# 64x64 output blocks, halved score masks and a scaling on GpSimd in a planned attention and MoE kernel

## Chip, cores, metric

One core of a Trainium2 chip runs the whole kernel. The metric is the device time of one execution in microseconds (us). The kernel before took 293.16 us, the median of three runs (292.2 to 295.71).

## What is computed

The reference chains three layers. First comes linear attention with decay, in blocks of 64 positions, for 2 batches, 8 heads, 768 positions and head size 64:

```python
for b in range(nb):                       # 12 blocks of 64
    intra = (qb @ kb.T * Dmask) @ vb      # Dmask: lam^(i-j) where i >= j, else 0
    inter = (qb * lam_pow) @ kv_state     # what earlier blocks left
    out[block] = intra + inter
    kv_state = lam**64 * kv_state + (kb * rev_pow).T @ vb
```

The scores of a block are masked only against keys of the same block; everything earlier comes through the 64x64 state of each head. Then follow `x = hardswish(x @ w_in) @ w_out` (512 to 2048 to 512, 1536 rows, the hidden rows are called g) and a soft mixture of 8 experts (`phi`, `w1`, `w2`) with two softmaxes over the logits `x @ phi`.

## The kernel before

**Attention tiles.** Twelve tiles t, six per batch, of 128 positions, that is, two chunks of 64. For each tile TensorE transposes q and k (`f_tr`, line 807, into PSUM `pt`), ScalarE copies both to SBUF `tr` (`f_ev`, line 824), and VectorE multiplies the transposed q, read from PSUM, by the powers of lambda `lamq` into `trd` (`f_trd`, line 830). The scores `ps` are 32 matmul records of 64x64 (`f_sc`, line 877). VectorE masks them in two instructions (`f_pm`, line 889): each score chunk is broadcast into both chunk columns and multiplied by `dec`, whose off-diagonal chunk is zero, so that `pm` holds 128 query columns per head and takes a whole buffer. GpSimd scales k (`f_kd`, line 863), TensorE forms the new states' products (`f_pv`, line 902), GpSimd decays the states (`f_sm`, line 947) and VectorE adds (`f_st`, line 960). The tile's output `px` (`f_px`) is 8 products of 128 keys by 64 by 128 queries (line 913; two records each) and then 16 small products with the states, 64x64 (line 921). ScalarE and VectorE split `px` into a high and a low part `x` (lines 938, 942).

**Matmul units.** 48 units (tile, quarter of `w_in`), 12 matmuls each of 128x512 (`h_unit`, line 1038), then ScalarE (line 1052) and VectorE (line 1058) make g. `w_in` and `w_out` arrive as 64-bit numbers and are converted by ScalarE and VectorE (lines 599 to 649; the low parts of two quarters by GpSimd, line 649). g reaches its transposed form through a VectorE transpose (line 1121) and four transfers from SBUF to SBUF (`f_move`, line 1131, tiles gq) for 5 of the 6 tile pairs.

**The end.** 64 transfers of 512 KB bring the experts' weights e (lines 1341, 1351, 1365); TensorE multiplies them as they land (lines 1559, 1593), and the rows of the output are formed (line 1662), copied and stored.

**Order.** Nothing is scheduled at run time. Every piece of work is an `op` with a number; `ORDER` lists all 974 numbers, and each engine runs its own in that order (`Plan.run`). The DMA transfers are issued in that order too, nearly all by SyncE (SP); those in `BY_ACT` by ScalarE. SBUF consists of 50 buffers of 4 KB per partition; each is handed from op to op by the plan, so a transfer of e waits at the head of SP's queue until the work that still reads its buffer is done. The sums in the plan (`cost`, `SWITCH`) choose which freed buffer an op gets.

Of the kernel before, what the change touches and what calls it, by code (L numbers as in the profile page):

```python
# [258 lines left out]
def attn_moe_softmoe_kernel(  # L259
# [237 lines left out]
    for item in CFG["loads"].split():
        i = int(item[1:])
        if item[0] in "qkv":
            load_qkv(item[0], i)  # L500
        elif item[0] == "t":
            for x in "qkv":
                load_qkv(x, i)
        elif item[0] == "w":
            load_w_in(i // 4, i % 4)
        elif item[0] == "W":
            for kt in range(KT):
                load_w_in(i, kt)
        elif item[0] == "p":
            ops["phi"] = load(load_phi, 65536, eff=0.4)  # L510
        elif item[0] == "D":
            each = {"SP": 600, "ACT": 700, "POOL": 1300}[CFG["decq"]]
            ops["pw_d"] = load(
                store_pw, 8192, deps=[pw_done], rel=[rp_buf], eng=CFG["decq"],
                each=440 if CFG["decq"] == "SP" else 800, free=CFG["decq"] == "SP",
            )
            ops["dec"] = [
                load(
                    load_dec(g), KB512 / 4, deps=[ops["pw_d"], zero],
                    eff=0.5, rows=32, eng=CFG["decq"], each=each, free=CFG["decq"] == "SP",  # L520
                )
                for g in range(2)
            ]
        elif item[0] == "o":
            load_wo_raw(i)
        else:
            for kk in range(4 * i, 4 * i + 4):
                load_wo_raw(kk)
# [1208 lines left out]
```

## Time and profile before

| | |
|---|---|
| median of three runs | 293.16 us |
| profiled execution, device time | 292.0 us |
| its span in the trace | 290.2 us |
| granted TensorE clock, mean | 0.993 |
| TensorE busy | 271.1 us, 93% |
| VectorE busy | 200.4 us, 69% |
| ScalarE busy | 122.9 us, 42% |
| GpSimd busy | 43.0 us, 15% |
| moved by DMA | 78.49 MB, 270 GB/s over the span |

The span is what the trace covers; the device time holds 1.8 us more. The ends of matmuls are modelled and overlap their successors, so a TensorE that is shown busy throughout may still have short gaps; what a block of matmuls costs is read from start to start. DMA shares are means over 16 engines.

### The profile page before, as it was taken

To read this page: it belongs to the slowest core of one execution; us is meant where nothing else is said; L and a number is where in the kernel's file an instruction comes from. 1 tells how busy PE (TensorE), PEld (TensorE's weight loads), DVE (VectorE), ACT (ScalarE), POOL (GpSimd) and SP (SyncE) were. 2 spreads that over 40 slices of the span, in tenths; PEclk is the share of its full clock that TensorE was granted. 3 is DMA by queue.
4 is the path that set the end of the run, shared out by engine and by line. 5 is a ranking of instruction groups with operands and counts; after the bars stand their busy time and mean duration, and the time that the engine had idled before them with its cause. 6 is when DMAs were issued, how large, how long until landed. Compare 5 with 4: busy or idle time off the path is not lost.

```text
span 290.2 us, 8501 instructions
## 1 busy us (share of the span) xinstructions
PE 271.1 (93%) x3532; PEld 205.4 (71%) x3532; DVE 200.4 (69%) x336; ACT 122.9 (42%) x237; POOL 43.0 (15%) x58
## 2 busy tenths in 40 slices
PE   7897999999999999999999999989999987999880
PEld 7786788778777888876677566768776665577570
DVE  5688899999999999977995976886124232160152
ACT  3475789988676562021332041403213511111250
POOL 6145323803062100000100202000000000000000
PEclk9999999999999999999999999999999999999997
DMA  8999889998688775686857899999999999999987
GB/s 183 266 249 287 225 242 311 350 354 241 185 248 244 201 199 118 149 210 167 208 134 173 186 265 269 309 330 306 338 403 390 357 368 382 412 405 377 288 274 217
DMA packets 79350, 78.49 MB, mean 270 GB/s; under 512 B 42952, under 2 KB 68048, under 8 KB 79312
## 3 DMA queue, kind: packets, MB, share of 16 engines
q1 hardware_dynamic: 77088, 76.50, 86.9%
q10 hardware_dynamic: 2224, 1.45, 1.9%
q8 instruction: 28, 0.46, 0.7%
q14 instruction: 10, 0.08, 0.1%
HBM read 60.10 MB, written 3.15 MB: 218 GB/s over the span
## 4 chain that ended last, share of the span: by engine, by line
PE 57%; DVE 10%; DMA 9%; issue 3%; ACT 2%; SPq 1%; DVEq 0%; ACTq 0%
PE h L1038 31%; DMA e<-in_moe_w_dram 6%; PE lg L1144 4%; PE po L1593 4%; PE pd L1259 4%; PE p L1559 3%; DVE tmp_o L613 2%; DMA wraw<-in_moe_w_in_dram 2%; DVE wo_f L620 2%; PE px L913 1%; PE pg L1103 1%; DVE g L1058 1%; PE pt L807 1%; PE w2p L751 1%; PE pt L1662 1%
## 5 line engine op out<-in xcount | busy, mean ns | idle before, releaser
L1038 PE MATMUL h<-whi,x 128*128 128x512 f32 x384 | 122.5, 400 | 2.1 <-DVE g L1058 1.9
L1038 PEld LDWEIGHTS h<-whi,x 128*128 128x128 f32 x384 | 69.6, 188 | 19.5 <-DVE g L1058 4.0
L1038 PE MATMUL h<-wlo,x 128*128 128x512 f32 x192 | 75.0, 391 | 0.0
L1052 ACT ACTIVATE g<-h,half_b 128x512 f32<-128x512 f32 x48 | 33.0, 692 | 58.2 <-PE h L1038 44.5
L1058 DVE SCALAR_TENSOR_TENSOR g<-g,h 128x512 f32<-128x512 f32 x48 | 32.3, 679 | 20.1 <-ACT g L1052 20.0
L1038 PEld LDWEIGHTS h<-wlo,x 128*128 128x128 f32 x192 | 36.0, 188 | 8.0
L1121 DVE STREAM_TRANSPOSE gb<-g 128x1024 f32<-128x1024 f32 x20 | 40.5, 2038 | 1.5 <-PE pd L1259 0.8
L947 POOL TENSOR_TENSOR states<-states,lamq 128x256 f32<-128x256 f32 x20 | 14.0, 702 | 89.9 <-DVE states L960 44.0
L863 POOL TENSOR_TENSOR vd<-qk,rev 128x512 f32<-128x512 f32 x12 | 13.5, 1128 | 40.4 <-DMA qk<-in_k_dram 16.0
L1593 PE MATMUL po<-e,ht 128*32 128x128 f32 (+1 forms) x384 | 16.6, 310 | 2.2 <-DMA e<-in_moe_w_dram 1.1
L1578 DVE STREAM_TRANSPOSE ht<-hsi 128x256 f32<-128x256 f32 x8 | 5.1, 646 | 19.5 <-ACT hsi L1570 19.5
L889 DVE TENSOR_TENSOR pm<-ps,dec 128x512 f32<-128x512 f32 x24 | 16.3, 680 | 1.7 <-DMA gq<-gb 1.4
L1559 PE MATMUL p<-e,hsi 128*32 128x256 f32 x256 | 15.9, 380 | 1.6 <-PE psi L1431 1.0
L824 ACT COPY tr<-pt 128x512 f32<-128x512 f32 x24 | 13.5, 586 | 7.4 <-DVE trd L830 3.9
L726 DVE STREAM_TRANSPOSE wb<-wo_f 128x1024 f32<-128x1024 f32 x8 | 16.4, 2049 | 0.1
L807 PE MATMUL pt<-ident,qk 128*128 128x128 f32 x96 | 15.6, 302 | 0.7 <-DMA qk<-in_q_dram 0.4
L1593 PEld LDWEIGHTS po<-e,ht 128*32 128x32 f32 x384 | 11.7, 110 | 6.0 <-DMA e<-in_moe_w_dram 1.6
L807 PEld LDWEIGHTS pt<-ident,qk 128*128 128x128 f32 x96 | 12.0, 153 | 4.3 <-issue 2.2
L1559 PEld LDWEIGHTS p<-e,hsi 128*32 128x32 f32 x256 | 9.1, 110 | 6.8 <-PE psi L1431 1.2
L620 DVE SCALAR_TENSOR_TENSOR tmp_i<-tmp_i 128x512 int32<-128x512 int32 x16 | 11.2, 708 | 3.2 <-ACT tmp_i L606 3.2
L620 DVE SCALAR_TENSOR_TENSOR wo_f<-tmp_o 128x512 int32<-128x512 int32 x16 | 13.3, 851 | 0.0
L913 PE MATMUL px<-pm,vd 128*64 128x128 f32 x192 | 13.1, 279 | 0.0
(116 smaller groups left out, 348.4 us busy)
## 6 DMA issues: line engine op xcount, KB each, us to landing
e<-in_moe_w_dram SPq DMA_DIRECT2D x64, 512.0 KB, 8.4
gq<-gb SPq DMA_DIRECT2D x72, 128.0 KB, 3.1
wraw<-in_moe_w_in_dram SPq DMA_DIRECT2D x16, 512.0 KB, 6.3
wo_raw<-in_moe_w_out_dram SPq DMA_DIRECT2D x16, 512.0 KB, 5.9
wq<-wb SPq DMA_DIRECT2D x32, 128.0 KB, 3.0
qk<-in_k_dram SPq DMA_DIRECT2D x24, 128.0 KB, 4.5
qk<-in_q_dram SPq DMA_DIRECT2D x24, 128.0 KB, 4.7
vd<-in_v_dram SPq DMA_DIRECT2D x12, 256.0 KB, 6.0
```

Of the source, the lines that this page charges most:

```text
L620: DVE.scalar_tensor_tensor(out=lw if dst is None else dst(), in0=hp, scalar=3, in1=lw, op0=ALU.logical_shift_left, op1=ALU.bitwise_or,)
L726: DVE.transpose(out=x.rearrange("p q d c f -> p c d q f"), in_=y.rearrange("p c (d t q) -> p c d q t", d=KT, q=4),)
L807: PE.transpose(p[:, a], x[:, i, 2 * a : 2 * a + 2].rearrange("p a d -> p (a d)"), ident,)
L889: DVE.tensor_tensor(out=T["pm", t][:, h], in0=T["ps", t][g][:, 0][:, :, None, :].broadcast_to((128, NPAIR, 2, Q)), in1=T["dec"][:, h], op= ...
L913: PE.matmul(px[kt // 2][rows(h2), kt % 2], lhsT=vd[:, 0, h], rhs=P[:, h], start=kt % 2 == 0, stop=False,)
L947: POOL.tensor_tensor(out=states[:, (n + 1) % 4], in0=states[:, n % 4], in1=T["lamq"][:, :, C - 1 : C].broadcast_to((128, NPAIR, Q)), op=AL ...
L1038: PE.matmul(ph, lhsT=xt[:, a, kt], rhs=T[w, n, part][:, kt % 2], start=i == 0, stop=i == 3 * KT - 1,)
L1052: ACT.activation(T["g", tp, n][:, i], T["h", t, n], AF.Relu, bias=half_b, scale=1.0 / 6.0)
L1058: DVE.scalar_tensor_tensor(out=to, in0=to, scalar=1.0, in1=T.pop(("h", t, n)), op0=ALU.min, op1=ALU.mult,)
L1121: DVE.transpose(out=x.rearrange("p q c i t -> p i c q t"), in_=T["g", tp, n].rearrange("p i (c t q) -> p i c q t", c=4, q=4),)
L1559: PE.matmul(p1[32 * j : 32 * j + 32], lhsT=T["sit"][:, b4], rhs=T["e1", e, b4][:, 256 * j : 256 * j + 256], start=b4 == 0, stop=b4 == 3,)
L1593: PE.matmul(T["po", hf][32 * qd : 32 * qd + 32], lhsT=T["ht", e // 4][:, e % 4, b8], rhs=T["e2", e, b8 // 2][:, b8 % 2, lo:hi] if e < WHOL ...
```

## The change

Five edits in the attention part, and a new order:

- `pm` holds only the equal chunks: 64 query columns per head instead of 128, one VectorE instruction of 128x256 per half instead of 128x512. It shares a buffer `tp` with `trd`; `dec` shares one with `lamq`. The zeroing of `dec` by GpSimd goes.
- `trd` is made by GpSimd from the SBUF copy `tr` instead of by VectorE from PSUM.
- In `f_px` the state products come first and open the accumulation; the 8 products of 128x64x128 become 16 of 64x64x64, in two halves of 8 with a drain of TensorE between them. In the first half the rows of the array match the rows used by the state products of the same PSUM tile; in the second they are the other ones.
- The two `dec` transfers wait for `lamq` (whose buffer they share) instead of for the zeroing. The ops `first`, `rev`, `lamq` are numbered ahead of the loads.
- `ORDER` is replaced (973 entries). With the shift in numbers undone (from 78 on, a number is one lower than before): SP starts with three of the four parts (512 KB each) of the first quarter of `w_in` and then k and q of tile 0, where it started with one part; two loads of e stand ahead of v and of k of tiles 9 and 10, and 16 loads of e instead of 14 stand ahead of the last transfers of gq; the products of tile 11's `px` and the first logits of pair 4 stand ahead of the units of tiles 8 and 9 in quarter 3; the logits of pair 3 stand behind seven units instead of behind the softmax sums of pair 2.

```diff
-            T["dec"] = bass.AP(
-                r.tensor, r.offset + Q - 1, [list(r.ap[0]), [2 * Q, H], [Q, 2], [-1, Q]]
-            )
+            T["dec"] = bass.AP(r.tensor, r.offset + Q - 1, [list(r.ap[0]), [Q, H], [-1, Q]])
...
-    zero = op("POOL", 1000, zero_dec, [pw_done], take=[ring_buf("dec")])
...
         def f_trd():
-            T["trd", t] = rtile([128, NPAIR, C], f"trd{t}")
-            DVE.tensor_tensor(out=T["trd", t], in0=T["pt", t, 0], in1=T["lamq"], op=ALU.mult)
+            T["tp", t] = rtile([128, 2, 512], f"tp{t}")
+            T["trd", t] = T["tp", t][:, 0].rearrange("p (a c) -> p a c", a=NPAIR)
+            POOL.tensor_tensor(
+                out=T["trd", t], in0=T["tr", t][:, 0], in1=T["lamq"], op=ALU.mult
+            )
...
-                if ("pm", t) not in T:
-                    T["pm", t] = rtile([128, H, 2, Q], f"pm{t}")
+                T["pm", t] = T["tp", t][:, 1].rearrange("p (h c) -> p h c", h=H)
                 h = slice(NPAIR * g, NPAIR * g + NPAIR)
                 DVE.tensor_tensor(
-                    out=T["pm", t][:, h],
-                    in0=T["ps", t][g][:, 0][:, :, None, :].broadcast_to((128, NPAIR, 2, Q)),
-                    in1=T["dec"][:, h], op=ALU.mult,
+                    out=T["pm", t][:, h], in0=T["ps", t][g][:, 0], in1=T["dec"][:, h],
+                    op=ALU.mult,
                 )
...
-            for kt in range(KT):
-                for h2 in range(2):
-                    h = 2 * kt + h2
-                    PE.matmul(
-                        px[kt // 2][rows(h2), kt % 2], lhsT=vd[:, 0, h], rhs=P[:, h],
-                        start=kt % 2 == 0, stop=False,
-                    )
+            first = 0 if c > 0 else 1
             for a in range(2):
-                for i in range(0 if c > 0 else 1, 2):
+                for i in range(first, 2):
                     for b in range(2):
                         for h2 in range(2):
                             PE.matmul(
                                 px[b][rows(h2), a, rows(i)],
                                 lhsT=states[rows(b), (2 * c + i) % 4, 2 * a + h2],
                                 rhs=T["trd", t][rows(b), 2 * a + h2, rows(i)],
-                                start=False, stop=a == i == 1,
+                                start=a == 0 and i == first, stop=False,
+                            )
+            for k in range(2):
+                if k:
+                    PE.drain()
+                for a in range(2):
+                    for b in range(2):
+                        for h2 in range(2):
+                            i, h = b ^ k, NPAIR * b + 2 * a + h2
+                            PE.matmul(
+                                px[b][rows(h2), a, rows(i)], lhsT=vd[rows(i), 0, h],
+                                rhs=P[rows(i), h], start=False, stop=k == a == 1,
                             )
...
-                "DVE", 610, f_trd, [tq, ops["lamq"]], prio, take=[b_trd], rel=[b_q, bufs["lamq"]]
+                "POOL", 1010, f_trd, [eq, ops["lamq"]], prio, take=[b_trd], rel=[b_tr, bufs["lamq"]]
...
-        pm0 = op("DVE", 600, f_pm(0), [sc] + ops["dec"], prio, take=[b_pm], rel=[b_s])
+        pm0 = op("DVE", 345, f_pm(0), [sc, trd] + ops["dec"], prio, rel=[b_s])
```

## Rows read from the trace of the kernel before

**Rows 1.** The page's part 1: busy us, share of the span and instructions
```profile
PE 271.1 (93%) x3532; PEld 205.4 (71%) x3532; DVE 200.4 (69%) x336; ACT 122.9 (42%) x237; POOL 43.0 (15%) x58
```

**Rows 2.** Chain of waits in time order: start us, us, engine, output, line
```profile
90.60 0.58 DVE g L1058
...
91.22 11.36 PE h L1038 x48
...
137.83 0.57 PE lg L1144 x8
...
164.66 2.70 DMA gq<-gb
...
168.07 0.70 DVE g L1058
...
271.74 6.80 DMA e<-in_moe_w_dram
```

**Rows 3.** Stretches: busy us of PE, PEld, DVE, ACT, POOL; clock, DMA share, GB/s
```profile
20.00:91.00 71.00, 67.83 (x980) 54.53 (x980) 67.93 (x114) 57.50 (x103) 26.32 (x25) 1.00 0.91 269
51.60:110.00 58.40, 56.78 (x678) 45.18 (x672) 57.74 (x85) 42.68 (x73) 17.18 (x15) 1.00 0.84 250
91.00:164.50 73.50, 73.28 (x814) 54.80 (x818) 65.74 (x81) 22.84 (x44) 5.30 (x7) 1.00 0.72 175
204.50:278.50 74.00, 69.28 (x1038) 48.47 (x1037) 20.92 (x58) 19.56 (x44) 0.00 (x0) 1.00 1.01 365
```

**Rows 4.** TensorE timeline around tile 8's scores and output: start us, us
```profile
110.05 0.69 PE L877 MATMUL ps<-tr 64*64 64x64 f32 x32
110.56 0.65 PE L902 MATMUL ps<-vd 64*64 64x64 f32 x32
111.14 1.10 PE L751 MATMUL w2p<-wq,phi_b 128*32 128x64 f32 x64
...
117.84 1.09 PE L913 MATMUL px<-pm,vd 128*64 128x128 f32 x16
...
119.49 1.10 PE L751 MATMUL w2p<-wq,phi_b 128*32 128x64 f32 x64
```

**Rows 5.** Weight loads of tile 8's state products; idle before in brackets
```profile
118.86 0.56 PEld L921 LDWEIGHTS px<-trd,states 64*64 64x64 f32 x32 [0.17 <-issue]
```

**Rows 6.** Groups of instructions: busy us, mean ns, idle before and releaser
```profile
L889 DVE TENSOR_TENSOR pm<-ps,dec 128x512 f32<-128x512 f32 x24 | 16.3, 680 | 1.7 <-DMA gq<-gb 1.4 <-PE ps L877 0.2
L942 DVE TENSOR_TENSOR x<-px,x 128x256 fp32r<-128x256 f32 x24 | 8.9, 412 | 1.3 <-ACT x L938 1.3
L830 DVE TENSOR_TENSOR trd<-pt,lamq 128x512 f32<-128x512 f32 x12 | 8.1, 676 | 2.9 <-ACT tr L824 2.8
L863 POOL TENSOR_TENSOR vd<-qk,rev 128x512 f32<-128x512 f32 x12 | 13.5, 1128 | 40.4 <-DMA qk<-in_k_dram 16.0 <-DMA gq<-gb 10.8 <-DMA qk<-in_q_dram 5.3
L613 DVE TENSOR_SCALAR tmp_o<-wo_raw 128x512 uint16<-128x512 uint16 x16 | 11.1, 698 | 0.0
L620 DVE SCALAR_TENSOR_TENSOR wo_f<-tmp_o 128x512 int32<-128x512 int32 x16 | 13.3, 851 | 0.0
```

**Rows 7.** The last two groups: ns min/median/max, first and last start us
```profile
L613 DVE TENSOR_SCALAR tmp_o<-wo_raw x16: 433/466/1621, 51.6 to 106.2; 128x512 uint16<-128x512 uint16 x16
L620 DVE SCALAR_TENSOR_TENSOR wo_f<-tmp_o x16: 640/680/1557, 53.2 to 109.7; 128x512 int32<-128x512 int32 x16
```

**Rows 8.** Timeline near 57 us: GpSimd's block and the slowest line 613
```profile
52.96 5.70 POOL L649 TENSOR_TENSOR wlo<-tmp_i,whi 128x512 fp32r<-128x512 f32 x4
57.37 1.62 DVE L613 TENSOR_SCALAR tmp_o<-wo_raw 128x512 uint16<-128x512 uint16 x1
```

**Rows 9.** First transposes, first unit, last transfers of gq: start us, us
```profile
7.15 1.09 PE L807 MATMUL pt<-ident,qk 128*128 128x128 f32 x4 [0.42 <-DMA qk<-in_q_dram]
20.53 0.71 PE L1038 MATMUL h<-whi,x 128*128 128x512 f32 x2
201.94 2.49 SPq L1131 DMA_DIRECT2D gq<-gb  x4
```

More of the change, by code (lines that the diff above doesn't have):

```diff
@@ L73 @@
 ORDER = (
[49 rows of a table removed]
[49 rows of a table added]
 )
-BY_ACT = (7, 9, 654, 674, 949,)
+BY_ACT = (11, 656, 659, 693, 948, 969, 972,)
 class Buf:
@@ L479, in fn @@
         def fn():
-            r = T["dec_r"]
+            r = T["dl"][:, 1].rearrange("p (h c) -> p h c", h=H)
             QUEUE[plan.eng].dma_start(
-                out=r[Q * g : Q * g + Q, :, g],
+                out=r[Q * g : Q * g + Q],
                 in_=bass.AP(pw_d.tensor, pw_d.offset, [[1, Q], [2 * Q, H], [1, Q]]),
             )
-            T["dec"] = bass.AP(
-                r.tensor, r.offset + Q - 1, [list(r.ap[0]), [2 * Q, H], [Q, 2], [-1, Q]]
-            )
-        return fn
-    def zero_dec():
-        T["dec_r"] = rtile([128, H, 2, Q], "dec")
-        POOL.memset(T["dec_r"], 0.0)
-    zero = op("POOL", 1000, zero_dec, [pw_done], take=[ring_buf("dec")])
+            T["dec"] = bass.AP(r.tensor, r.offset + Q - 1, [list(r.ap[0]), [Q, H], [-1, Q]])
+        return fn
     rp_buf = Buf("R", 1, (1,))
[L497 to L506, printed above, removed]
-            for kt in range(KT):
[L508 to L515, printed above, removed]
-            )
[L517 to L528, printed above, removed]
     def lamq_products():
@@ L550, in make_lamq @@
     def make_lamq():
-        T["lamq"] = rtile([128, NPAIR, C], "lamq")
+        T["dl"] = rtile([128, 2, 512], "dl")
+        T["lamq"] = T["dl"][:, 0].rearrange("p (a c) -> p a c", a=NPAIR)
         DVE.tensor_copy(
@@ L581, in attn_moe_softmoe_kernel @@
     )
+    for item in CFG["loads"].split():
+        i = int(item[1:])
+        if item[0] in "qkv":
+            load_qkv(item[0], i)
+        elif item[0] == "t":
+            for x in "qkv":
+                load_qkv(x, i)
+        elif item[0] == "w":
+            load_w_in(i // 4, i % 4)
+        elif item[0] == "W":
+            for kt in range(KT):
+                load_w_in(i, kt)
+        elif item[0] == "p":
+            ops["phi"] = load(load_phi, 65536, eff=0.4)
+        elif item[0] == "D":
+            each = {"SP": 600, "ACT": 700, "POOL": 1300}[CFG["decq"]]
+            ops["pw_d"] = load(
+                store_pw, 8192, deps=[pw_done], rel=[rp_buf], eng=CFG["decq"],
+                each=440 if CFG["decq"] == "SP" else 800, free=CFG["decq"] == "SP",
+            )
+            ops["dec"] = [
+                load(
+                    load_dec(g), KB512 / 4, deps=[ops["pw_d"], ops["lamq"]],
+                    eff=0.5, rows=32, eng=CFG["decq"], each=each, free=CFG["decq"] == "SP",
+                )
+                for g in range(2)
+            ]
+        elif item[0] == "o":
+            load_wo_raw(i)
+        else:
+            for kk in range(4 * i, 4 * i + 4):
+                load_wo_raw(kk)
     def conv_reserve(p):
@@ L792, in attention @@
         last = c == NC - 1
-        b_tr, b_trd, b_pm = Buf("R"), Buf("R"), Buf("R")
+        b_tr, b_trd = Buf("R"), Buf("R")
         q_tag, k_tag = "gl" if t < CFG["early"] else "ss"
@@ L828, in f_trd @@
         def f_trd():
-            T["trd", t] = rtile([128, NPAIR, C], f"trd{t}")
-            DVE.tensor_tensor(out=T["trd", t], in0=T["pt", t, 0], in1=T["lamq"], op=ALU.mult)
+            T["tp", t] = rtile([128, 2, 512], f"tp{t}")
+            T["trd", t] = T["tp", t][:, 0].rearrange("p (a c) -> p a c", a=NPAIR)
+            POOL.tensor_tensor(
+                out=T["trd", t], in0=T["tr", t][:, 0], in1=T["lamq"], op=ALU.mult
+            )
         def f_tb():
@@ L855, in f_td @@
         def f_td():
-            T["trd", t] = rtile([128, NPAIR, C], f"trd{t}")
+            T["tp", t] = rtile([128, 2, 512], f"tp{t}")
+            T["trd", t] = T["tp", t][:, 0].rearrange("p (a c) -> p a c", a=NPAIR)
             DVE.tensor_tensor(
@@ L907, in f_px @@
         def f_px():
-            vd, P = T["vd", t], T["pm", t].rearrange("p h i c -> p h (i c)")
+            vd, P = T["vd", t], T["pm", t]
             px = T["px", t] = [ptile("xg"[b], [128, 2, C], f"px{t}_{b}") for b in range(2)]
-            for kt in range(KT):
-                for h2 in range(2):
-                    h = 2 * kt + h2
-                    PE.matmul(
-                        px[kt // 2][rows(h2), kt % 2], lhsT=vd[:, 0, h], rhs=P[:, h],
-                        start=kt % 2 == 0, stop=False,
-                    )
+            first = 0 if c > 0 else 1
             for a in range(2):
-                for i in range(0 if c > 0 else 1, 2):
+                for i in range(first, 2):
                     for b in range(2):
@@ L924, in f_px @@
                                 rhs=T["trd", t][rows(b), 2 * a + h2, rows(i)],
-                                start=False, stop=a == i == 1,
+                                start=a == 0 and i == first, stop=False,
+                            )
+            for k in range(2):
[8 more added lines that the diff above has]
+                                rhs=P[rows(i), h], start=False, stop=k == a == 1,
                             )
@@ L993, in attention @@
         ek = op("ACT", 480, f_ev(1), [tk, first], prio, rel=[b_k])
-        sc = op("PE", 560, f_sc, [eq, ek], prio, take=[b_s], rel=[b_tr], mode="S")
+        sc = op("PE", 475, f_sc, [eq, ek], prio, take=[b_s], rel=[b_tr], mode="S")
         ops["sc", t] = sc
-        pm0 = op("DVE", 600, f_pm(0), [sc] + ops["dec"], prio, take=[b_pm], rel=[b_s])
-        pm1 = op("DVE", 600, f_pm(1), [pm0], prio, rel=[b_s, bufs["dec"]])
+        pm0 = op("DVE", 345, f_pm(0), [sc, trd] + ops["dec"], prio, rel=[b_s])
+        pm1 = op("DVE", 345, f_pm(1), [pm0], prio, rel=[b_s, bufs["lamq"]])
         kd = op(
-            "POOL", 1060, f_kd, [ops["ldk", t], ops["rev"]], prio,
+            "POOL", 1010, f_kd, [ops["ldk", t], ops["rev"]], prio,
             rel=[b_qk, b_vd],
@@ L1002, in attention @@
         pv = op(
-            "PE", 300 if last else 560, f_pv, [kd, ops["ldv", t], sc], prio, rel=[b_vd], mode="S"
+            "PE", 240 if last else 475, f_pv, [kd, ops["ldv", t], sc], prio, rel=[b_vd], mode="S"
         )
@@ L1011, in attention @@
                 free = op(
-                    "POOL", 700, f_sm(i), [state[-1], free, ops["lamq"]], prio,
+                    "POOL", 600, f_sm(i), [state[-1], free, ops["lamq"]], prio,
                     rel=[bufs["lamq"]],
                 )
-            state.append(op("DVE", 440, f_st(i), [free, pv], prio, rel=[b_s]))
+            state.append(op("DVE", 335, f_st(i), [free, pv], prio, rel=[b_s]))
         px = op(
-            "PE", 1450 if c > 0 else 1170, f_px, [pm1, ops["ldv", t], trd] + state[:2], prio - 0.1,
-            take=b_x, rel=[b_vd, b_pm, b_states, b_trd], mode="VS",
-        )
-        xh = op("ACT", 610, f_xh, [px], prio - 0.2, take=[ring_buf(("x", t))])
-        ops["x", t] = op("DVE", 740, f_xl, [xh], prio - 0.2, rel=b_x)
+            "PE", 1120 if c > 0 else 890, f_px, [pm1, ops["ldv", t], trd] + state[:2], prio - 0.1,
+            take=b_x, rel=[b_vd, b_states, b_trd], mode="S",
+        )
+        xh = op("ACT", 535, f_xh, [px], prio - 0.2, take=[ring_buf(("x", t))])
+        ops["x", t] = op("DVE", 670, f_xl, [xh], prio - 0.2, rel=b_x)
         if not last:
```

98 rows, old and new, of the table ORDER are left out of this document.

## The prediction, made before the changed kernel was run

> **What bounds the kernel now.** I read the page's busy shares first: TensorE is busy 93% of the span, VectorE 69%, GpSimd 15% [rows 1]. A mean over the span says little, so the chain of waits comes second. Up to 91 us it runs over VectorE (its last piece there starts at 90.60); from 91.22 it is TensorE nearly without a break, but for a stall from 164.66 to 168.8 (a transfer of gq, then ScalarE and VectorE); at the end it is the transfers of the experts' weights e, the last of which lands at 271.74 + 6.80 = 278.54 [rows 2]. The stretches come third. From 20 to 91 us both are full: TensorE 67.83 of 71.0 us, VectorE 67.93. From 91 to 164.5 TensorE is busy 73.28 of 73.5 and DMA only 0.72. From 204.5 to 278.5 DMA is at 1.01 and 365 GB/s, whoever else waits [rows 3]. So there are three stages: TensorE with VectorE, TensorE alone, DMA. A microsecond saved ahead of 200 us counts only if the weights' transfers start earlier by it, and inside the last stage only fewer bytes count.
>
> **The products of px on TensorE.** Tile 8's output takes 119.49 - 117.84 = 1.65 us from start to start, the change of array shape inside it included [rows 4]; that change is the 0.17 us idle ahead of the state products [rows 5]. Afterwards the block is 64 records of 64x64, 32 for states and 32 for the products. Their price is the scores': 32 records in 110.56 - 110.05 = 0.51 us [rows 4], so 1.02, and 0.07 to leave the shape (the next 32 took 111.14 - 110.56 = 0.58). The drain is not in the trace; it cannot gain. The nearest row is the idle time at a change of shape, 0.17 [rows 5]; I take 0.19, a little over it, and keep 0 and twice the row, 0.34, for emptying and refilling. That makes 1.28 us, a saving of 0.37 (0.22 to 0.56) for each of 12 tiles, 4.4 us in all. Tiles 0 and 6 have half the state products, with no other answer.
>
> **VectorE.** A mask of 128x256 with one operand in PSUM should last what the low part x lasts, 0.412 us, against 0.680 now; scaling q takes 0.676 and leaves VectorE [rows 6]. A tile gives back 2 x 0.268 + 0.676 = 1.21 us, 12 tiles 14.6. Between 20 and 91 us there are 14 masks and 6 scalings: 7.8 us.
>
> **GpSimd.** Scaling q there costs about what scaling k does, 1.128 us for the same 128x512 [rows 6], 12 times 13.5 us; GpSimd has the room. But VectorE pays: shifts that take 0.466 and 0.680 at the median average 0.698 and 0.851 [rows 6, 7], and the longest, 1.62, ends just as GpSimd's four subtractions end [rows 8]. That excess, 16 x (0.232 + 0.171) = 6.4 us, falls in a stretch in which GpSimd is busy 17.2 [rows 3], so 0.37 us for each us of GpSimd. Six new scalings of 1.128 us cost VectorE 2.5 of its 7.8; 5.3 remain. SBUF - State Buffer in the Trainium skill (Who interferes with whom) says more: the pair of ports that both share is an exclusive lock, and the loser waits for the whole instruction. By it each scaling could hold VectorE for all of its 1.128 us, and six would take 6.8 of the 7.8; the row with 1.62 us agrees with that for one instruction, the averages do not for all. That is a rival below.
>
> **The stage up to 91 us.** TensorE saves 7 x 0.37 = 2.6 there; VectorE would allow 5.3, and TensorE's own idle time of 3.2 us [rows 3] sets the ceiling at 5.8. I take 4.0, between the first two.
>
> **From 91 us to the last gq.** Three px save 1.1. The stall of 4.1 us [rows 2]: the logits that waited for gq now stand behind seven units, which hides that wait, but the new order may pay for it elsewhere; I take 2.0 (0 to 4.1). Tile 11's px and four rows of logits now stand ahead of the units whose g goes last: 1.28 + 0.57 [rows 2] = 1.85 us later.
>
> **The start.** k and q of tile 0 are behind two more 512 KB transfers: 1.05 MB at 269 GB/s [rows 3] is 3.9 us on the first transposes at 7.15. The two mask transfers now wait for `lamq`; behind them on SP stand v of tile 1 and q, k, v of tile 2, and with them those tiles' first steps. On the other side the first unit at 20.53 [rows 9] finds its weights converted, and VectorE has less to do. Bounds -1 to +3.9; I take +1.0, nearer the lower since 13 us lie between the transposes and that unit. Zeroing `dec` is off the path and costs nothing either way; if the masks waited for it, at most what GpSimd spends on a scaling of k.
>
> **The last stage.** In the order, 16 loads of e instead of 14 stand ahead of the last transfers of gq (201.94 [rows 9]); the buffers for it come from `pm` and `dec`, which need none of their own. The remaining 50 took 74.0 us at a DMA share of 1.01 [rows 3], 1.48 each; two fewer save 3.0 (0 if they only displace others in the queue).
>
> **Sum.** -4.0 - 1.1 - 2.0 + 1.85 + 1.0 - 3.0 = -7.25. The span of 290.2 becomes 283.0; 1.8 us lie around it, so 284.8 for an execution like the profiled one of 292.0, which stands 1.2 below the median of 293.16. **Forecast: 286.0 us**, 2.4% under that median.
>
> **Rivals.**
> - **The transfers hide it.** SP's queue is in order and the e loads wait for buffers that the late units free; if only the two advanced loads count, 293.2 - 3.0 = 290.2; if those displace others, 293. For: DMA share 0.95 and more from there on. Against: DMA has room at 0.72 just before [rows 3], where earlier work can put bytes.
> - **The port lock takes VectorE's gain** up to 91 us. Then 7.8 - 6.8 = 1.0 us of slack is all that TensorE is given, and with a stall kept the sum is -1.0 - 1.1 + 1.85 + 1.0 - 3.0 = -2.3: 290.9.
> - **Slower: GpSimd's queue becomes the path.** In the new order the scaling of q of tiles 0 to 3 stands between k's scaling and the decay of states, right ahead of the masks, which share its buffer; VectorE made it beside the copies. If each of the 12 tiles is later by its 1.128 us, 13.5 us against -7.25 gives +6.2: 299.4. It decides once the scaling ends after the second mask. Against: GpSimd idles 45 of 71 us up to 91 [rows 3].
> - **More than forecast.** TensorE gets the ceiling of 5.8, the whole stall goes and the start costs nothing: -5.8 - 1.1 - 4.1 + 1.85 - 3.0 = -12.2, so 281.0.
>
> That the drain leaves no saving at all in px (its drain would have to last 0.56, three times the idle time at a change of shape) lies inside the first rival.
>
> **How the numbers follow.** Chances: forecast 0.52 (283.5 to 288.5), hidden by transfers 0.18, lock 0.11, more 0.11, GpSimd's queue 0.08. The forecast case carries the bounds of stall, start and drain, about 2.5 us each way. 2%, about what a measurement of this kernel can tell from no change, begins at 287.3 below and 299.0 above. Of the forecast case three quarters, 0.39, are under 287.3; with the case of more that is 0.50. Slower than 299.0 is most of the queue case, 0.06; the rest is 0.44. Range 281.5 to 292.5: it leaves out the queue case, about half of the case of more and a little of the hidden one, some 0.17.
>
> **What would show it.** Start-to-start time of a px block near 1.28 us; masks near 0.41 and scalings near 1.1; lines 613 and 620 with a higher mean; TensorE's idle time from 20 to 91 us below 3.2; first unit near 21.5; last gq near 197.7; last e landing near 271. Wrong, if px stays above 1.45, if masks wait for GpSimd, or if the last gq moves and the last landing doesn't.

## The result, and the profile after

The changed kernel takes 289.83 us (median of 20 runs, 287.56 to 294.08), the kernel before in the same series 293.91 us: a ratio of 0.9856 with a 95% interval of 0.983 to 0.9881, 1.4% faster. The forecast was 286.0 us. Ratios, here and below, leave out executions in the slower of two states in which the program can run; medians don't. The profiled execution took 289.83 us, with a span of 288.0.

Part 1 of the page, the answer to [rows 1]:

```profile
PE 265.4 (92%) x3724; PEld 200.5 (70%) x3724; DVE 188.1 (65%) x324; ACT 121.9 (42%) x237; POOL 60.7 (21%) x69
```

VectorE lost 12.3 us, GpSimd gained 17.7, TensorE lost 5.7. The stretches, as in [rows 3], with the same columns:

```profile
20.00:91.00 71.00, 65.43 (x1110) 53.13 (x1111) 61.67 (x107) 53.20 (x96) 38.93 (x34) 1.00 0.93 265
91.00:164.50 73.50, 72.08 (x825) 53.79 (x823) 62.94 (x76) 24.59 (x46) 5.46 (x6) 1.00 0.73 191
204.50:278.50 74.00, 70.87 (x1069) 49.00 (x1067) 21.95 (x62) 20.40 (x48) 0.00 (x0) 1.00 1.01 377
```

From 20 to 91 us VectorE is no longer full, but TensorE stands idle for 5.6 us instead of 3.2. What VectorE was spared is not used there. What TensorE waits for in that stretch (line, releaser, us in total, times, longest; the three largest; "issue" is a wait with no releaser in the profile):

```profile
PE ps L892 <- issue: 3.5, 4, 1.6
PE h L1033 <- DVE g L1053: 0.8, 2, 0.5
PE ps L869 <- issue: 0.4, 1, 0.4
```

The groups of instructions that answer to [rows 6]:

```profile
L880 DVE TENSOR_TENSOR tp<-ps,dl 128x256 f32<-128x256 f32 x24 | 9.5, 415 | 10.2 <-issue 3.9 <-PE ps L892 3.3 <-PE ps L869 2.1
L819 POOL TENSOR_TENSOR tp<-tr,dl 128x512 f32<-128x512 f32 x12 | 17.1, 1426 | 33.0 <-ACT tr L812 15.0 <-DMA gq<-gb 7.2 <-DVE wo_f L608 5.6
L855 POOL TENSOR_TENSOR vd<-qk,rev 128x512 f32<-128x512 f32 x12 | 14.3, 1192 | 37.6 <-DMA gq<-gb 17.6 <-DMA qk<-in_k_dram 12.8 <-DVE rev L504 7.3
L608 DVE SCALAR_TENSOR_TENSOR wo_f<-tmp_o 128x512 int32<-128x512 int32 x16 | 13.0, 828 | 0.2
```

A mask (line 880) lasts 0.415 us as forecast; the scaling of q (line 819) 1.43, not 1.13. No mask waits for a scaling: the waits ahead of masks are for products of TensorE, for one transfer and, 3.9 us at 179.03, for something without a name, 9 us after that tile's scaling was done. TensorE's timeline around tile 7's output, for [rows 4], and its weight loads, for [rows 5]:

```profile
86.14 0.70 PE L905 MATMUL px<-tp,states 64*64 64x64 f32 x32
86.65 0.99 PE L918 MATMUL px<-tp,vd 64*64 64x64 f32 x32
87.57 0.65 PE L739 MATMUL w2p<-wq,phi_b 128*32 128x64 f32 x31
```

```profile
87.17 0.33 PEld L918 LDWEIGHTS px<-tp,vd 64*64 64x64 f32 x16 [0.24 <-issue]
```

The block takes 87.57 - 86.14 = 1.43 us, 0.22 less than before; the 0.24 us idle ahead of its last 16 products is where the drain stands. First transposes, first unit and last gq (from the timelines of TensorE and SP, for [rows 9]), and the last landing in the chain of waits:

```profile
10.40 1.94 PE L795 MATMUL pt<-ident,qk 128*128 128x128 f32 x8 [4.09 <-DMA qk<-in_q_dram]
...
21.93 0.71 PE L1033 MATMUL h<-whi,x 128*128 128x512 f32 x2
```

```profile
204.38 2.55 SPq L1126 DMA_DIRECT2D gq<-gb  x4
```

```profile
259.57 17.41 DMA e<-in_moe_w_dram x2
```

The last gq is issued 2.4 us later than before, yet the last e lands at 259.57 + 17.41 = 276.98, 1.6 us earlier. Within this profile all of the gain is behind the last gq.

### The profile page after: what moved, and what is told of

It is laid out like the page before. It is cut to its first block, busy times and chain, and to the rows that moved or that the text cites. A ratio compares the mean times of both kernels' runs of the same rounds, so it can differ in the third digit from the quotient of the medians.

```text
span 288.0 us, 8892 instructions
## 1 busy us (share of the span) xinstructions
PE 265.4 (92%) x3724; PEld 200.5 (70%) x3724; DVE 188.1 (65%) x324; ACT 121.9 (42%) x237; POOL 60.7 (21%) x69
## 4 chain that ended last, share of the span: by engine, by line
PE 53%; DMA 16%; DVE 13%; SPq 7%; issue 5%; ACT 2%; ACTq 2%; DVEq 0%
PE h L1033 28%; DMA e<-in_moe_w_dram 10%; DMA gq<-gb 5%; PE pd L1254 3%; DVE wb L714 3%; PE lg L1139 3%; SPq L1126 3%; PE pt L795 3%; PE px L918 2%; DVE g L1053 2%; SPq L428 2%; DVE gb L1116 2%; PE px L905 2%; PE ps L892 2%; ACTq L1126 2%
## 5 line engine op out<-in xcount | busy, mean ns | idle before, releaser
L1047 ACT ACTIVATE g<-h,half_b 128x512 f32<-128x512 f32 x48 | 33.1, 689 | 64.3 <-PE h L1033 42.8
L942 POOL TENSOR_TENSOR states<-states,dl 128x256 f32<-128x256 f32 x20 | 14.8, 741 | 51.3 <-DVE states L955 29.5
L819 POOL TENSOR_TENSOR tp<-tr,dl 128x512 f32<-128x512 f32 x12 | 17.1, 1426 | 33.0 <-ACT tr L812 15.0
L855 POOL TENSOR_TENSOR vd<-qk,rev 128x512 f32<-128x512 f32 x12 | 14.3, 1192 | 37.6 <-DMA gq<-gb 17.6
L795 PE MATMUL pt<-ident,qk 128*128 128x128 f32 x96 | 14.2, 289 | 4.7 <-DMA qk<-in_q_dram 4.3
L795 PEld LDWEIGHTS pt<-ident,qk 128*128 128x128 f32 x96 | 11.4, 147 | 7.3 <-DMA qk<-in_q_dram 4.2
L880 DVE TENSOR_TENSOR tp<-ps,dl 128x256 f32<-128x256 f32 x24 | 9.5, 415 | 10.2 <-issue 3.9
L1554 PE MATMUL p<-e,hsi 128*32 128x256 f32 x256 | 15.3, 381 | 0.5 <-DVE hsi L1449 0.3
L1588 PEld LDWEIGHTS po<-e,ht 128*32 128x32 f32 x384 | 11.1, 110 | 6.7 <-issue 1.9
L608 DVE SCALAR_TENSOR_TENSOR tmp_i<-tmp_i 128x512 int32<-128x512 int32 x16 | 12.7, 798 | 2.8 <-ACT tmp_i L594 2.6
L892 PE MATMUL ps<-vd 64*64 64x64 f32 x352 | 9.1, 230 | 3.9 <-issue 3.5
```

The lines of the kernel that those rows point to most:

```text
L608: DVE.scalar_tensor_tensor(out=lw if dst is None else dst(), in0=hp, scalar=3, in1=lw, op0=ALU.logical_shift_left, op1=ALU.bitwise_or,)
L795: PE.transpose(p[:, a], x[:, i, 2 * a : 2 * a + 2].rearrange("p a d -> p (a d)"), ident,)
L819: POOL.tensor_tensor(out=T["trd", t], in0=T["tr", t][:, 0], in1=T["lamq"], op=ALU.mult)
L892: PE.matmul(ps[i][rows(g), 1, p], lhsT=vd[rows(i), 1, 2 * p + g], rhs=vd[rows(i), 0, NPAIR * g + p], start=True, stop=True,)
L942: POOL.tensor_tensor(out=states[:, (n + 1) % 4], in0=states[:, n % 4], in1=T["lamq"][:, :, C - 1 : C].broadcast_to((128, NPAIR, Q)), op=AL ...
L1047: ACT.activation(T["g", tp, n][:, i], T["h", t, n], AF.Relu, bias=half_b, scale=1.0 / 6.0)
```

## The experiments

All ratios are to the kernel before, timed beside each kernel. Unless said otherwise the edit is against the changed kernel. Three groups: which part of the change makes the time (first five), what the parts that did not go as forecast cost (next four), and the order (last three).

**1. The edits in the old order.**

```diff
 ORDER = (
-    16, 288, 290, 289, 1, 291, 15, 14, 282, 7, 9, 17, 284, 8, 0, 4, 292, 11, 276, 2,
+    1, 0, 14, 4, 7, 9, 6, 11, 78, 8, 15, 276, 277, 2, 278, 10, 279, 280, 281, 16,
...
```

> The changed kernel in the order of the kernel before (five steps moved behind what they now read; the start, the place of the units and the 14 loads of e ahead of the last gq are the old ones). Theory A, the gain is the last stage's, which the new order gives by 16 loads of e ahead of the last gq instead of 14: then the edits alone are worth at most TensorE's 12 x 0.22 = 2.6 us on px, and this kernel takes 291.3 to 294, the last landing of e at about 277 to 279. Rival B, the edits themselves make the gain (TensorE's shorter px and VectorE's relief) and the order only follows them: 288.5 to 290, the last gq earlier than 201.9 by 3 us or more. Either way px should last 1.43 us from start to start and the masks 0.41, as in the changed kernel.

Measured 292.55 us, ratio 0.9972 (0.9929 to 1.0015): no gain that can be told from none. By the time that is theory A, but the last gq is issued at 206.10, 4.2 us later than before, which neither theory had, and experiment 2 shows theory A to be wrong.

**2. The same, with q scaled on VectorE from PSUM as before,** so that only px and the masks are changed.

```diff
-            POOL.tensor_tensor(
-                out=T["trd", t], in0=T["tr", t][:, 0], in1=T["lamq"], op=ALU.mult
+            DVE.tensor_tensor(
+                out=T["trd", t], in0=T["pt", t, 0], in1=T["lamq"], op=ALU.mult
...
-                "POOL", 1010, f_trd, [eq, ops["lamq"]], prio, take=[b_trd], rel=[b_tr, bufs["lamq"]]
+                "DVE", 610, f_trd, [tq, ops["lamq"]], prio, take=[b_trd], rel=[b_q, bufs["lamq"]]
```

> The edits in the old order (292.55 with all three), but q scaled on VectorE from PSUM as before, so that only px and the masks differ from the kernel before. Theory P (in the old order GpSimd's scaling costs VectorE about what it takes off: the shifts' lines lasted 50.9 us in all there, 45.3 before and 44.0 in the changed kernel, VectorE 196.1 us busy of the hoped-for 186): the shifts fall back to about 45, VectorE stays at 194 to 197, the time at 291.5 to 293.5. Rival G (the move is worth its 2 us in any order, as in the new one): 294.5 or more.

Measured 287.23 us, ratio 0.9798 (0.9749 to 0.9846): the fastest kernel of the study, and ahead of both theories. Two of the three main edits, in the old order, save 2.0%; moving q to GpSimd there takes 1.7% back. Chain, last gq (timeline of SP) and stretch of this kernel:

```profile
266.88 7.20 DMA e<-in_moe_w_dram
```

```profile
198.37 2.52 SPq L1126 DMA_DIRECT2D gq<-gb  x4
```

```profile
20.00:91.00 71.00, 67.34 (x1101) 54.05 (x1102) 67.62 (x119) 57.57 (x104) 28.10 (x26) 1.00 0.93 275
```

Last gq 3.6 us and last landing (274.08) 4.5 us earlier than before. The same stretch of experiment 1, and its last gq:

```profile
20.00:91.00 71.00, 65.03 (x1078) 52.08 (x1079) 65.15 (x103) 54.92 (x100) 36.48 (x31) 0.95 0.87 259
```

```profile
206.10 2.50 SPq L1126 DMA_DIRECT2D gq<-gb  x4
```

With q on GpSimd TensorE stands 6.0 us instead of 3.7, and its mean granted clock is 0.95. Where this comes from is read from the shifts of the conversions on VectorE, in experiment 1 and then in experiment 2 (groups, as above):

```profile
L608 DVE SCALAR_TENSOR_TENSOR tmp_i<-tmp_i 128x512 int32<-128x512 int32 x16 | 16.1, 1018 | 2.8 <-ACT tmp_i L594 2.6
L608 DVE SCALAR_TENSOR_TENSOR wo_f<-tmp_o 128x512 int32<-128x512 int32 x16 | 14.3, 911 | 1.5 <-ACT tmp_o L594 1.5
```

```profile
L608 DVE SCALAR_TENSOR_TENSOR tmp_i<-tmp_i 128x512 int32<-128x512 int32 x16 | 12.0, 757 | 3.1 <-ACT tmp_i L594 2.9
L608 DVE SCALAR_TENSOR_TENSOR wo_f<-tmp_o 128x512 int32<-128x512 int32 x16 | 11.7, 753 | 0.5 <-ACT tmp_o L594 0.5
```

With line 601 the shifts last 50.9 us in all against 44.2. VectorE's busy time is 196.1 against 194.3 although 8.2 us of scaling have left it, so 18.0 us more of GpSimd cost VectorE 10.0. In the new order the shifts do not grow so: they last 44.0 us in the changed kernel and 42.8 to 45.6 in experiments 4, 5, 8, 9 and 10, which share its order but for the start in 8 and 9.

Two places in experiment 1 make up what the stage up to 91 us loses. The first, on GpSimd, on VectorE, then on TensorE, then the stretches around it:

```profile
54.09 6.10 POOL L637 TENSOR_TENSOR wlo<-tmp_i,whi 128x512 fp32r<-128x512 f32 x4 [1.33 <-DMA wo_raw<-in_moe_w_out_dram]
```

```profile
53.57 2.38 DVE L608 SCALAR_TENSOR_TENSOR tmp_i<-tmp_i 128x512 int32<-128x512 int32 x2
55.87 1.53 DVE L601 TENSOR_SCALAR tmp_o<-wo_raw 128x512 uint16<-128x512 uint16 x1
57.29 0.67 DVE L1053 SCALAR_TENSOR_TENSOR g<-g,h 128x512 f32<-128x512 f32 x1
```

```profile
58.01 1.10 PE L1033 MATMUL h<-whi,x 128*128 128x512 f32 x2 [2.48 <-DVE g L1053]
...
62.23 0.39 PE L1033 MATMUL h<-wlo,x 128*128 128x512 f32 x1
62.45 0.63 PE L1033 MATMUL h<-whi,x 128*128 128x512 f32 x2
```

```profile
58.00:60.00 2.00, 1.99 (x5) 1.62 (x6) 2.00 (x4) 1.11 (x2) 2.00 (x2) 0.54 1.14 325
60.00:62.00 2.00, 2.00 (x7) 1.54 (x7) 2.00 (x6) 0.00 (x0) 0.18 (x1) 0.60 1.09 387
```

GpSimd's block here is four subtractions of the conversions, not a scaling of q. Beside it the two shifts of line 608 take 2.38 us and the one of line 601 takes 1.53; in experiment 2, where the two stand ahead of the block, the same three take 1.27 and 1.54. So g comes late, TensorE waits 2.48 us, and then runs for almost 4 us at a granted clock of 0.54 to 0.60, that is, mostly at 1.2 instead of 2.4 GHz. That costs another 2 x (0.46 + 0.40) = 1.7 us. In experiment 2 TensorE waits 0.98 us for g at the same unit, and its clock row stays at 1.00. The second place, on TensorE, with a stretch behind it:

```profile
26.38 0.69 PE L892 MATMUL ps<-vd 64*64 64x64 f32 x32 [1.81 <-POOL states L942]
```

```profile
28.00:30.00 2.00, 2.00 (x8) 1.52 (x7) 0.00 (x0) 0.34 (x1) 0.00 (x0) 0.50 1.30 251
```

The profile names GpSimd's decay of states; GpSimd works there from 20.86 on without a pause, a scaling of q among the rest, and without that scaling, in experiment 2, the same products have waited 1.28 us. The clock rows from 26 to 32 us are 0.86, 0.50 and 0.78, 1.7 us more; in experiment 2 they say 1.00. Longer waits (0.5 + 1.5) and clock (1.7 + 1.7) make 5.4 us, and px of tile 7 starts at 88.67 in experiment 1 and at 83.49 in experiment 2, 5.2 us apart. This compares one execution of each, of 294.14 and 287.46 us; the medians are 5.3 us apart.

**3. Each mask issued twice,** to price VectorE's time.

```diff
-                DVE.tensor_tensor(
-                    out=T["pm", t][:, h], in0=T["ps", t][g][:, 0], in1=T["dec"][:, h],
+                for _ in range(2):
+                    DVE.tensor_tensor(
+                        out=T["pm", t][:, h], in0=T["ps", t][g][:, 0], in1=T["dec"][:, h],
...
```

> The changed kernel with each of the 24 masks issued twice, into the same place: 24 x 0.41 = 9.9 us more of VectorE, 5.8 of it between 20 and 91 us, a little more than the masks had cost before. Theory V (from 20 to 91 us VectorE still sets the pace, 61.7 of 71 us busy, and its relief is passed on): 293 to 295. Rival (VectorE has the room now): 289 to 291, VectorE's busy time near 198.

Measured 296.73 us, ratio 1.0126 (1.008 to 1.0172), beyond theory V's upper end. Its page, part 1:

```profile
PE 267.1 (90%) x3724; PEld 200.3 (68%) x3724; DVE 200.9 (68%) x348; ACT 121.7 (41%) x237; POOL 59.9 (20%) x69
```

The masks' group grew from 9.5 to 19.7 us; the time by 1.0126 - 0.9856 = 2.7%, 7.9 us. Each us of VectorE put on at the masks costs about 0.8. The change takes 16.3 - 9.5 = 6.8 us off them; that a us taken off is worth as much is not shown.

**4. Four drains for one,** which undoes px's saving on TensorE.

```diff
-                    PE.drain()
+                    for _ in range(4):
+                        PE.drain()
```

> The changed kernel with each of its 12 drains issued four times; a second one cost 0.08 us, so a px block should last 1.43 + 3 x 0.08 = 1.67 us, what it lasted before (1.65): the saving on TensorE is undone and nothing else. Theory A (TensorE's 0.22 us per tile is hidden by waits): within 0.7 of 289.8. Rival B (TensorE's time is passed on): 12 x 0.24 = 2.9 us more, 292.5.

Measured 290.49 us, ratio 0.9838 (0.9785 to 0.989), with a block of 1.65 us: theory A. TensorE's 12 x 0.22 = 2.6 us change the time by -0.5 us, give or take 1.7 (from both intervals); in this order they are not seen.

**5. Two drains for one,** run ahead of it.

```diff
                     PE.drain()
+                    PE.drain()
```

> The changed kernel with the drain of each of the 12 px blocks issued twice. It prices the drain and TensorE's time ahead of the last gq. If a drain lasts by itself what the idle time behind it shows, a px block grows from 1.43 to about 1.67 us; if the second finds nothing to wait for, to 1.5 or less. Where TensorE's time ahead of the last gq passes into the end one to one, 12 x 0.24 = 2.9 us more: 292.7. Theory A (what TensorE saved was lost to waits, so that a little more of it is hidden by them too): within 1 us of 289.8 though the block grows.

Measured 290.47 us, ratio 0.9866 (0.9828 to 0.9905): theory A. The block is 86.94 - 85.43 = 1.51 us (timeline of TensorE, tile 7):

```profile
85.43 0.69 PE L905 MATMUL px<-tp,states 64*64 64x64 f32 x32
85.95 0.41 PE L919 MATMUL px<-tp,vd 64*64 64x64 f32 x16
86.55 0.46 PE L919 MATMUL px<-tp,vd 64*64 64x64 f32 x16 [0.19 <-issue]
86.94 0.77 PE L739 MATMUL w2p<-wq,phi_b 128*32 128x64 f32 x40
```

A second drain, of an empty engine, costs 0.08 us. The first one is put at 0.34, the changed kernel's block of 1.43 less the forecast's 1.02 + 0.07 for the records; no run is without it.

**6. q scaled on VectorE in the new order,** from SBUF, in GpSimd's place.

```diff
-            POOL.tensor_tensor(
+            DVE.tensor_tensor(
                 out=T["trd", t], in0=T["tr", t][:, 0], in1=T["lamq"], op=ALU.mult
```

> The changed kernel with the scaling of q on VectorE instead of GpSimd, same operands, same place in the order. Rival C (VectorE's relief is the gain): VectorE gets 12 x about 0.68 = 8.1 us back, half of it between 20 and 91 us, and the time rises by 2 to 4 us, to 292 to 294. Theory A, with what the shared ports cost: GpSimd loses 12 x 1.43 = 17 us of work, VectorE's shifts shorten by about 0.37 us for each of these, 6.3 us, and the time stays at 288.8 to 290.8, VectorE's busy time about 190.

Measured 296.83 us, ratio 1.0103 (1.0062 to 1.0144), more than either theory. VectorE's queue and then TensorE's:

```profile
153.92 0.69 DVE L819 TENSOR_TENSOR tp<-tr,dl 128x512 f32<-128x512 f32 x1 [4.17 <-DMA gq<-gb]
```

```profile
155.27 1.22 PE L1033 MATMUL h<-whi,x 128*128 128x512 f32 x2 [4.46 <-DVE g L1053]
```

**7. The same, each scaling just ahead of its first mask.**

```diff
-    243, 509, 510, 712, 706, 511, 722, 504, 505, 254, 506, 248, 512, 713, 246, 718, 707, 513, 507, 709,
+    243, 509, 510, 712, 706, 511, 722, 504, 505, 254, 506, 248, 512, 713, 718, 707, 513, 507, 709, 708,
...
+    516, 719, 517, 249, 253, 691, 75, 514, 76, 246, 250, 255, 789, 515, 714, 717, 720, 256, 77, 251,
...
```

(246 is tile 10's scaling.)

> As the last kernel (q scaled on VectorE from SBUF), which took 296.83, but each scaling put directly ahead of its tile's first mask on VectorE's queue. Theory Q (the 7 us were one wait in VectorE's queue: the scaling of a late tile waited 4.17 us for a buffer of gq, the g behind it came late and TensorE stood still 4.46 us at 150 us; on GpSimd nobody stands behind such a wait): that wait goes and 290 to 292.5 remain. Theory C (VectorE's 9 us of work are the price wherever they stand): 295 to 297.

Measured 294.17 us, ratio 0.9934 (0.989 to 0.9979), which is 292.0 of 293.9: by the ratio theory Q, while the median lies between both theories. Some 1.7% was the wait in an ordered queue; beyond it, the move to GpSimd gains 0.8% in the new order, where it costs 1.7% in the old. The two are not quite the same move: here VectorE reads q from SBUF, in experiment 2 from PSUM, and no run has the new order with q read from PSUM.

**8. k and q of tile 0 first again.**

```diff
-    16, 288, 290, 289, 1, 291, 15, 14, 282, 7, 9, 17, 284, 8, 0, 4, 292, 11, 276, 2,
+    16, 7, 9, 288, 290, 289, 1, 291, 15, 14, 282, 17, 284, 8, 0, 4, 292, 11, 276, 2,
```

> The changed kernel with k and q of tile 0 second on SP's queue again, ahead of two of the weights' loads (two numbers of the order moved, nothing else). Theory S (the new order's start costs time: the first transposes at 10.40 us instead of 7.15, TensorE at 0.50 to 0.76 of its clock from 7 to 16 us): first transposes near 7.2, granted clock 1.00 throughout, the last gq 1 to 2.5 us earlier and the time 287.3 to 288.8. Rival (the first unit waits for converted weights, not for tile 0; what is gained at 7 us is lost at 20): first unit within 0.5 us of 21.9 or later, time 289.5 to 291.

Measured 291.0 us, ratio 0.9873 (0.982 to 0.9925): the rival. The transposes came at 7.52, but the scores then waited for ScalarE's copies, which stand behind conversions of weights that now land later (timeline of TensorE):

```profile
7.52 1.06 PE L795 MATMUL pt<-ident,qk 128*128 128x128 f32 x8 [1.16 <-DMA qk<-in_q_dram]
8.42 0.61 PE L520 MATMUL keep_on<-ident 128*128 128x128 f32 x4
14.15 1.13 PE L869 MATMUL ps<-tr 64*64 64x64 f32 x32 [5.12 <-ACT tr L812]
```

**9. TensorE kept busy while it waits for tile 0.**

```diff
-    fill={'first': 8, 'k0': 2, 'k1': 6, 'lg': 1, 'lr': 4, 'pd': 3},
+    fill={'first': 8, 'k0': 2, 'k1': 6, 'rev': 14, 'lg': 1, 'lr': 4, 'pd': 3},
...
+        keep_on(CFG["fill"]["rev"])
```

> The changed kernel with 14 more products of 128x128 without use on TensorE behind the product for k's scaling, so that TensorE stands still for half a us instead of 4.1 us ahead of the first transposes. Theory S (the idle time costs TensorE its clock: the 32 scores of tile 0 last 1.13 us at 13 us and 0.65 at 19): the block lasts 0.65, px of tile 0 starts 2 to 2.5 us earlier than 17.9, and the time falls to 287.5 to 289. Rival (from 15 us on tile 1's q and v and the weights set the pace): px of tile 0 moves by less than 0.5 us, or the time stays at 289.3 to 290.5.

Measured 289.88 us, ratio 0.9837 (0.976 to 0.9914): the rival. The scores of tile 0 do last 0.69 us instead of 1.13, but what follows waits for v and q (timeline of TensorE):

```profile
12.38 0.69 PE L872 MATMUL ps<-tr 64*64 64x64 f32 x32 [0.28 <-ACT tr L815]
14.41 0.70 PE L895 MATMUL ps<-vd 64*64 64x64 f32 x32 [1.33 <-DMA vd<-in_v_dram]
15.79 1.06 PE L798 MATMUL pt<-ident,qk 128*128 128x128 f32 x8 [0.68 <-DMA qk<-in_q_dram]
```

px of tile 0 starts at 18.12 against 17.90. Theory S had a second fault: in the kernel before, the same fill products of tile 0 last as long (4 in 1.06 us from 9.60) though its clock row says 1.00, so the slow start was not new.

**10. Two loads of e moved behind the last gq.**

```diff
-    581, 562, 829, 797, 563, 584, 585, 741, 582, 583, 860, 586, 612, 613, 795, 783, 866, 587, 731, 742,
+    581, 562, 829, 797, 563, 584, 585, 741, 582, 583, 860, 586, 612, 613, 866, 587, 731, 742, 795, 783,
```

> The changed kernel with two loads of e moved from ahead of the last transfers of gq to behind them (14 ahead instead of 16, nothing else). Theory A (each load of e that stands ahead of the last gq is one fewer of 1.46 us behind it): the last gq stays within 1 us, the last landing is 2.9 us later, the time 292.7. Rival (the transfers run at their full share from 185 us on anyway, so that two loads ahead only displace gq and others): the last gq comes 2 to 3 us earlier, the last landing stays within 1 us, the time 289.8.

Measured 289.79 us, ratio 0.9875 (0.9831 to 0.9918): the rival. The last gq is issued 2.7 us earlier and the last e lands at 258.72 + 17.58 = 276.30 instead of 276.98:

```profile
201.71 2.64 SPq L1126 DMA_DIRECT2D gq<-gb  x4
```

```profile
258.72 17.58 DMA e<-in_moe_w_dram x2
```

**11. The kernel before with the new order's last stage** (against the kernel before).

```diff
-    713, 714, 689, 672, 690, 698, 691, 722, 244, 70, 723, 253, 716, 701, 704, 502, 705, 839, 247, 246,
-    717, 255, 511, 512, 503, 504, 706, 799, 715, 248, 707, 249, 513, 514, 517, 719, 518, 515, 516, 521,
...
+    713, 714, 689, 672, 690, 698, 691, 722, 244, 70, 723, 253, 716, 701, 704, 502, 705, 858, 247, 246,
+    717, 255, 511, 512, 503, 504, 706, 839, 715, 248, 707, 249, 513, 514, 517, 719, 518, 515, 516, 521,
...
```

> The kernel before (old px, old masks, q on VectorE, old order), but the loads of e, the last transposes, psi, the experts' products and the output follow one another as in the new order, in the places that such steps had in the old one (14 loads still ahead of the last gq). Theory D (the 1.2% that the new order gives beside the edits lies in the last stage: from 220 to 270 us the kernel before moves 381 GB/s, the changed one 400, since its loads of e never stand behind one that waits for a buffer): rate 395 or more there, the last landing 2 to 3 us after nothing else has moved, 290 to 291.5. Rival E (the gain lies ahead of 200 us, in what runs beside what): rate and landing as before, 293 to 294.5.

Measured 297.36 us, ratio 1.0146 (1.0095 to 1.0198). It moves 397 GB/s from 220 to 270 us, as theory D wants, and is slower all the same: its last gq is issued at 205.62, 3.7 us later than before, so this run cannot tell what the rate alone is worth. Experiment 1 can tell more, with the old order's last stage (stretches):

```profile
220.00:270.00 50.00, 46.98 (x801) 33.00 (x804) 15.41 (x48) 12.90 (x31) 0.00 (x0) 1.00 1.03 405
```

It moves 405 GB/s there, the changed kernel 400 and experiment 2 385, and has no gain: a high rate there is not the new order's own, and a kernel can have it and gain nothing. Theory D falls by that. Rival E's time was missed as well; what is left of it is that the gain lies ahead of 200 us.

**12. Half a unit between scores and state products,** tiles 2 to 6.

```diff
-    23, 108, 297, 106, 107, 116, 298, 33, 119, 109, 120, 26, 299, 36, 110, 485, 121, 113, 122, 117,
+    23, 108, 297, 106, 107, 116, 298, 33, 119, 109, 26, 299, 36, 110, 485, 120, 121, 113, 122, 117,
...
```

> The changed kernel with half a unit's six products moved between scores and state products of tiles 2 to 6 (five swaps on TensorE's queue), so that no 128 records of 64x64 stand back to back. Theory I (the idle times inside homogeneous blocks, 0.77, 0.63, 0.40 and 1.60 us with no releaser, come every 126 records or so, as often as 16 KB of instructions are fetched: px of 64 short records instead of 48 longer ones runs ahead of that fetch): these idle times shrink from 3.4 us to under 1; five more changes of shape cost about 5 x 0.3 = 1.5; time 288 to 289.5, and TensorE's idle time from 20 to 91 us falls from 5.6 us. Rival (the state products wait there for GpSimd or a transfer, which the trace does not name): the idle times stay at the same products or move to the next, time 290 to 292.

Measured 294.02 us, ratio 1.0012 (0.9974 to 1.005), slower than either theory. The idle times inside blocks of one kind and without a named releaser did shrink, to 0.22 us, but others took their place (timeline of TensorE):

```profile
28.06 0.59 PE L1033 MATMUL h<-whi,x 128*128 128x512 f32 x1 [2.34 <-issue]
...
69.60 0.33 PE L892 MATMUL ps<-vd 64*64 64x64 f32 x4 [1.47 <-DVE tp L880]
```

So what those idle times are is left open; removing them is not worth a worse order.

**Together.** Medians and ratios of the kernels with the new px and masks:

| | old order | new order |
|---|---|---|
| q on VectorE | 287.23, 0.9798 (0.9749 to 0.9846) | 294.17, 0.9934 (0.989 to 0.9979) |
| q on GpSimd | 292.55, 0.9972 (0.9929 to 1.0015) | 289.83, 0.9856 (0.983 to 0.9881) |

The new order's place for VectorE's q is that of experiment 7, which reads it from SBUF.

## Why the forecast came out as it did

The sign was right and the time inside the range, 3.8 us above the forecast; of the steps, several were wrong, and that the total lies as near as it does is in part luck. TensorE's idle time up to 91 us, the last gq and the last landing (276.98 instead of about 271) all missed what the forecast named as its signs. The first rival's 290.2 is nearer, but its reason, that the two advanced loads of e count, is refuted too (experiment 10).

- **px.** Forecast 1.28 us, measured 1.43: the term mis-sized is the drain, some 0.34 us instead of 0.19, the upper of the bounds kept for it. The saving of 0.22 us per tile is not seen in the time in the new order (experiment 4). How much of the 5.9 us of experiment 2 is px's was not separated.
- **VectorE.** Masks as forecast, and this is likely the part that pays: at the 0.8 per us of experiment 3, 6.8 us would give some 5.3, an estimate that takes time off to be worth what time put on costs.
- **GpSimd.** The forecast let VectorE pay 0.37 us for each us. In the order that it was made for VectorE paid less: without masks and scaling it was busy about 200.4 - 16.3 - 8.1 = 176.0 us before and 188.1 - 9.5 = 178.6 after, 2.6 us for 17.7 of GpSimd, that is 0.15. In the old order the shifts alone paid (50.9 - 44.2) / 18.0 = 0.37, and all of VectorE's lines together 10.0 / 18.0 = 0.56, more than the scaling had cost there. So the second rival's claim, that VectorE's gain by q is taken back, is met in the old order and not in the new. The third rival, GpSimd's queue as the path, shows at one place of the old order (26.38 in experiment 1) and at no mask of the changed kernel. SBUF — State Buffer in the Trainium skill (SBUF: two separate sides) says that of VectorE's operations only those in a two-port mode or with two SBUF inputs compete for the shared pair. The rows agree: line 608 goes up to 1.79 us beside GpSimd (1.78 at 78.42, beside a scaling of q at 78.18 that lasts 1.47), while the masks, which read PSUM, stay within 0.375 to 0.426 in the same run, experiment 1.
- **Up to 91 us.** Forecast -4.0; the step that failed is the overlap. VectorE did get the room, 61.67 us busy instead of 67.93, 6.3 less where the forecast had 5.3 left; but TensorE did not use it, and its idle time rose from 3.2 to 5.6 us. Of these 0.8 are waits for g and some 4 have no named releaser; what those are stays open (experiment 12). The clock row of this stretch is 1.00, so in this profile the clock is no part of it. In the old order the step fails otherwise: px and masks alone bring px of tile 7 from 84.84 to 83.49, and with q on GpSimd it goes to 88.67, because TensorE waits for late results and then runs at a lower clock, which the forecast did not price.
- **The start.** +3.25 us on the first transposes (bound +3.9), +1.4 on the first unit (forecast +1.0). Experiments 8 and 9 show that mending it gains nothing.
- **From 91 us to the last gq.** Forecast 197.7, measured 204.38. This step failed by 6.7 us; the 4.0 that the stage before should have brought were already missing, and 2.7 are what experiment 10 gives back: the two loads of e that stand ahead of gq delay it, for which the forecast charged nothing.
- **The last stage.** From last gq to last landing 72.6 us instead of 76.6, about the 3.0 us forecast; but the reason given, two loads of e ahead, is refuted by experiment 10. They displace gq, as the first rival said: transfers run at a share of 1.0 there, and what counts is the bytes left. Why the last stage moves 377 GB/s instead of 365 is not settled; experiment 1, in the old order, moves 381 in the same stretch.

What the new order does, then, is take back 1.2% of the 1.7% that GpSimd's scaling costs in the old one. That it does so by what stands beside what ahead of 200 us is supported by VectorE's price for GpSimd's time, 0.15 instead of 0.56, and by elimination after experiments 10 and 11; no run moves such a meeting alone. In the changed kernel's profile one remains, read from VectorE's timeline:

```profile
59.27 3.45 DVE L608 SCALAR_TENSOR_TENSOR wo_f<-tmp_o 128x512 int32<-128x512 int32 x2
62.64 1.27 DVE L1053 SCALAR_TENSOR_TENSOR g<-g,h 128x512 f32<-128x512 f32 x2
```

Two shifts take 3.45 us beside GpSimd's subtractions and g follows late. TensorE is idle from 62.85 to 64.45; the profile names no releaser here, but in experiments 4, 8 and 9, which share the order, the wait of 1.6 to 1.9 us at this place is for g, and the granted clock falls behind it. In experiment 10, which shares it too, the two shifts take 2.37 us and TensorE does not wait there, so the meeting differs from execution to execution.

## What to carry to other kernels

Time each part of a compound change in the order it is to run in: here two edits gave 2.0%, a third took 1.7% back, and a new order hid most of that. An operation moved to an engine that shares ports with the one relieved is priced by what runs beside it, and by the third engine that waits for the result. Bytes issued earlier gained nothing here, where the transfers were already full.
